# Signs of three pairs written as two halves side by side, and one pair's turns at slot 73

## The chip, the cores and the metric

One core of one Trainium2 chip. The metric is the device time of one execution in microseconds (us). Three runs of the kernel before took 329.01, 328.08 and 329.04 us, median 329.01. The engines are TensorE (PE, matrix products), VectorE (DVE), ScalarE (ACT), GpSimd (POOL) and SyncE (SP), which here only issues DMA transfers.

## What is computed

Attention under a hash mask, then a gated feed-forward layer on its result. In the reference, cut to what matters:

```python
q_bits = (einsum('bhsd,dk->bhsk', q, proj) > 0)      # 6 bits for each row; k_bits the same
mask = q_bucket[:, :, :, None] == k_bucket[:, :, None, :]
scores = where(mask, q @ k.T / sqrt(D), -1e9)
attn = softmax(scores) @ v                           # B=4, H=8, S=768, D=64
xn = rmsnorm(attn as rows of 512) * rms_g
out = (silu(xn @ w_gate) * (xn @ w_val)) @ w_out     # d_ff = 1536
```

The kernel writes the mask as arithmetic. Behind the 64 values of each k and q column of the tile QK stand 12 rows of bits, scaled so that one product over 76 rows gives the score of a pair of rows with equal buckets and a very negative number for all others.

## The kernel before

**Windows, pairs and slots.** The 3072 rows of the result are taken as eight windows w of 384 rows (batch b = w // 2). Heads go in pairs hp, so (b, hp) names the data of two heads. The work of attention is a list of 192 slots: one slot is one pair of score matmuls (`scores`, s_ps) and its exponentials on ACT (`probs`). Windows 0 to 3 take the pairs in the order of `TURNS`; the pairs of batch 1 come to their scores in the order (1,0), (1,1), (1,2), (1,3), six slots each, once for window 2 and once for window 3.

**The plan.** Everything else is entered by hand into a slot with `at(slot, function, ..., rank=...)`. The last loop walks through the slots, issues the scores of the next slot, and then the entries of this slot in the order of their rank (3 unless given). Each engine, and SP's queue of DMA issues, works through its own instructions in the order in which this loop issued them. An instruction that must wait holds up all that stand behind it on its engine.

**The feed-forward part of window w** begins at slot 24 w + 42: twelve gate steps (`gate`, g_ps, four matmuls and a tanh on ACT) and twelve value steps (`value`, v_ps, four matmuls and two DVE instructions t and ht) over 16 slots, then nine steps of the last product (`project`, y_ps). The tiles d_ps, g_ps, v_ps, m_ps, x_ps and y_ps go round three PSUM banks (pool `gps`): each allocation waits until the third one before it has been read.

**How q and k get to QK.** The first six pairs (`BY_PE`) are turned by PE. The others are loaded in blocks of 32 (`load_blocks`, four transfers for each of kL and qL, issued by SP) and turned by DVE in eight steps (`turn_dve`, L205: four of kT, then four of qT, one slot each, rank 5). `cast_pool` (L213) copies them to the rows 0 to 63 of QK on POOL.

**The hash.** `hash_bank` multiplies up to four 384-column blocks by the projection, each into its own strip of 32 partitions of one bank (d_ps, L221). `signs` (L228) turns a bank to bits on DVE, into a tile bits with three buffers. SP then sends rows of 12 partitions to the rows 64 to 75 of QK:

- `hash_heads` (slot 40 for pair (1,1)): strips are k and q of the first head, then of the second; `move` sends eight transfers (L279).
- `hash_lone` (slot 58 for (1,2), slot 65 for (1,3)): strips are k and q of the first half of the columns, then of the second; `send` issues four transfers for each head (L297), for (1,2) the second four at the end of slot 59.
- `hash_pairs` for two pairs of batch 2 or 3, two banks; pairs (2,0) and (2,1) at slot 82. It already writes the halves side by side and sends whole rows (L319).

**What else SP issues here:** the transposes of xn to xnT (`turn_x`, L458), the loads of q, k and v (L127, L117) and the stores of the result (L514).

**The table `work`** gives, for each pair turned by DVE, the slots of its loads of k, q and v, the first slot s of its eight turns, and the slot of its hash. The casts follow at s + 4 and s + 8, `v_prep` and `v_sum` at s + 9, and for (2,1) two slots later. Pair (2,1) has loads at 66, 67 and 68, turns from 74, hash at 82.

Of the kernel before, what the change touches and what calls it, by code (L numbers as in the profile page):

```python
# [9 lines left out]
FP16 = mybir.dt.float16  # L10
AF = mybir.ActivationFunctionType
ALU = mybir.AluOpType
# [4 lines left out]
S = 768  # L17
D = 64
# [3 lines left out]
HALF = 384  # L22
KROWS = D + 12
# [25 lines left out]
def kernel(  # L49
# [12 lines left out]
    nc = tc.nc  # L62
# [9 lines left out]
    spool = ctx.enter_context(tc.tile_pool(name="spool", bufs=2))  # L72
# [12 lines left out]
    thr = const.tile([128, 1], FP32, name="thr")  # L85
    scl = const.tile([128, 1], FP32, name="scl")
# [45 lines left out]
    T0, QK = {}, {}  # L132
# [16 lines left out]
    def t0(b, h, which):  # L149
        hp, hh = divmod(h, 2)  # L150
        return T0[b, hp, which][:, hh * HALF : (hh + 1) * HALF]
# [66 lines left out]
    def hash_bank(parts):  # L218
        ps = bank("d_ps", [128, HALF])
        for t, (w, src) in enumerate(parts):  # L220
            nc.tensor.matmul(  # L221
                ps[32 * t : 32 * t + 32, :], w, src,
                start=True, stop=True, tile_position=(0, 32 * t),
            )
        return ps

    def signs(bt, ps):
        nc.vector.tensor_scalar(  # L228
            out=bt, in0=ps, scalar1=thr, scalar2=scl, op0=ALU.is_gt, op1=ALU.mult
        )  # L230

    def bit_rows(b, h, t):
        return QK[b, h // 2][D:KROWS, h % 2, t * HALF : (t + 1) * HALF]

# [2 lines left out]
    def bits_tile(i):  # L237

        if i % 2 == 0:
            held.append(spool.tile([128, S], FP16, name="bits", bufs=3))  # L240
        return held[-1][:, (i % 2) * HALF : (i % 2 + 1) * HALF]

    def hash_head(h):


        kt, qt = t0(0, h, "k"), t0(0, h, "q")
        ps = hash_bank(
            [(pk[:, 0:32], kt), (pq[:, 0:32], qt), (pk[:, 12:44], kt), (pq[:, 12:44], qt)]
        )
        bt = bits_tile(h)  # L250
        signs(bt, ps)

        def move(movers, t0=0):
            for t, eng in enumerate(movers, t0):
                src = bt[32 * t : 32 * t + 12]
                if eng is nc.scalar:
                    nc.scalar.copy(bit_rows(0, h, t), src)
                elif eng is nc.sync:
                    eng.dma_start(out=bit_rows(0, h, t), in_=src)
                else:  # L260
                    eng.tensor_copy(bit_rows(0, h, t), src)

        return move

    def hash_heads(b, hp):

        ps = hash_bank(
            [(w[:, 0:32], t0(b, 2 * hp + hh, which))
             for hh in range(2) for w, which in ((pk, "k"), (pq, "q"))]
        )  # L270
        bt = bits_tile(0)
        signs(bt, ps)

        def move(eng, blocks):
            for hh, t in blocks:
                p0 = 64 * hh + 32 * (t % 2) + 12 * (t // 2)
                dst, src = bit_rows(b, 2 * hp + hh, t), bt[p0 : p0 + 12]
                if eng is nc.sync:
                    eng.dma_start(out=dst, in_=src)  # L279
                else:  # L280
                    eng.tensor_copy(dst, src)

        return move

    def hash_lone(b, hp):

        ps = hash_bank(
            [(w[:, 0:32], T0[b, hp, which][:, half * HALF : (half + 1) * HALF])
             for half in range(2) for w, which in ((pk, "k"), (pq, "q"))]
        )  # L290
        bt = bits_tile(0)
        signs(bt, ps)

        def send(hh):
            for half, j in ((0, 0), (0, 1), (1, 1), (1, 0)):
                p0, o = 64 * half + 32 * j + 12 * hh, (S, 0)[j] + half * HALF
                nc.sync.dma_start(  # L297
                    out=QK[b, hp][D:KROWS, hh, o : o + HALF], in_=bt[p0 : p0 + 12]
                )

        send(0)
        moves[b, hp] = send
# [324 lines left out]
    moves = {}  # L627
# [4 lines left out]

    def hash_pair(b, hp):
        moves[b, hp] = hash_heads(b, hp)
        odd = [(0, 2), (1, 2), (0, 3), (1, 3)]
        even = [(0, 0), (0, 1), (1, 0), (1, 1)]
        moves[b, hp](nc.sync, odd if b == 0 else even[:2] + odd[:1] + even[2:] + odd[1:])
# [17 lines left out]
    for hp, s, slots in ((2, 12, (13, 14, 15, 16)), (3, 17, (18, 19, 20, 21))):  # L655
        at(s, hash_pair, 0, hp)
        for i, s in enumerate(slots):
            at(s, lambda hp=hp, i=i: moves[0, hp](nc.vector, [divmod(i, 2)]), rank=5)
# [10 lines left out]
    for hp, loads, turns, sh, evens, sv in (  # L669
        (0, (9, 11, 13), (20, 21, 24, 27), 33, (41, 42), (27, 44)),  # L670
        (1, (13, 14, 36), (29, 31, 33, 35), 40, (45, 47), (49, 51)),
    ):
        for which, sl in zip("kqv", loads):
            at(sl, load_rows, nc.sync, 1, hp, which)
        for i, sl in enumerate(turns):
            at(sl, keep_pair, 1, hp, i)
            at(sl + 1, casts, 1, hp, i)
        at(sh, hash_pair, 1, hp)
        for hh, sl in enumerate(evens):
            at(sl, cast_half, 1, 2 * hp + hh, "q", 0)  # L680
        at(sv[0], v_prep, 1, hp)
        at(sv[1], v_sum, 1, hp)
# [3 lines left out]
    def in_row(loads, s, hash_slot=None):  # L686
        return loads, range(s, s + 8), (s + 4, s + 8, s + 9), hash_slot

    work = {
        (1, 2): in_row((31, 32, 45), 49, 58), (1, 3): in_row((41, 43, 50), 56, 65),  # L690
        (2, 0): in_row((53, 55, 60), 64), (2, 1): in_row((66, 67, 68), 74, 82),
        (2, 2): in_row((72, 75, 78), 82), (2, 3): in_row((79, 86, 87), 90, 99),
        (3, 0): in_row((88, 91, 98), 100), (3, 1): in_row((94, 97, 112), 110, 119),
        (3, 2): in_row((115, 118, 124), 126), (3, 3): in_row((122, 125, 137), 136, 145),
# [1 line left out]
    for (b, hp), (loads, turns, cast_slots, sh) in work.items():  # L696
        for which, s in zip("kqv", loads):
            at(s, load_rows if which == "v" else load_blocks, nc.sync, b, hp, which)
        for i, s in enumerate(turns):
            at(s, turn_dve, b, hp, "kq"[i // 4], i % 4, rank=5)  # L700
        for which, s in zip("kq", cast_slots):
            at(s, cast_pool, b, hp, which)
        if sh:
            later = {(1, 2): (59, 7), (2, 1): (86, 7)}.get((b, hp), (sh, 3))
            if b == 1:
                at(sh, hash_lone, b, hp)
            else:
                at(sh, hash_pairs, b, (hp - 1, hp))
            at(later[0], lambda b=b, hp=hp: moves[b, hp](1), rank=later[1])
        late = 2 if (b, hp) == (2, 1) else 0  # L710
        at(cast_slots[2] + late, v_prep, b, hp)
        at(cast_slots[2] + late, v_sum, b, hp)
        if b > 1 and hp % 2:
            at(48 * b + (17 if hp == 3 else -8), v_mean, b, hp - 1, 4)
# [27 lines left out]
    for w in range(8):  # L742
# [33 lines left out]
        for i in range(9 if w < 7 else 6):  # L776
            c, j = divmod(i, 3)
# [3 lines left out]
    for s in range(NS + 48):  # L781
# [3 lines left out]
        n = sum(r < 3 for r, _, _ in todo) if s < NS - 1 else 0  # L785
# [48 lines left out]
```

## Time and profile before

The profile is one execution taken by the hardware's profiler.

| | before |
|---|---|
| median of three runs | 329.01 us |
| the profiled execution | 328.34 us |
| its span in the trace | 326.6 us, 7743 instructions |
| PE busy | 98% of the span |
| DVE, ACT, POOL busy | 71%, 64%, 51% |
| granted clock of PE | 1.00 |
| chain that ended last | PE 92%, DVE 2%, ACT 2%, DMA 1% |

In a timeline a row is: start in us from the span's start, length in us, engine and line of the program, operation, the tile written <- the tiles read, shapes, and count; in brackets the idle time of the engine in front of it and what ended it. Rows with a count over 1 are merged, and neighbours on one engine can overlap a little. "SPq" is SP's queue of DMA issues: the length is that of the issue and not of the transfer. A row of the waits reads: engine, instruction <- what it waited for, then us in total, times, longest. A row of the windows has the stretch, its length, and for PE, weight loads, DVE, ACT and POOL the busy time with the number of instructions, then the granted clock, the share of the DMA engines and GB/s. A row for a tile has the line, engine, operation, count, and the shortest, median and longest duration in ns.

### The profile page before, as it was taken

The page shows a single profiled execution, that of the slowest core. Times are in us where ns is not written, and L with a number is a line of the kernel's source. Part 1 is how long each engine was busy: PE and PEld are TensorE (multiplying, and loading weights), DVE is VectorE, ACT ScalarE, POOL GpSimd, SP SyncE. Part 2 cuts the span into 40 slices and gives each one's busy share as a digit, 9 for nine tenths or more (in the row PEclk, how much of TensorE's full clock was granted, in tenths as well). Part 3 has the DMA queues.
Part 4 walks back from the last instruction along what each step waited for, and adds up shares of the span by engine and source line. Part 5 has one row for each costly group of instructions (what it writes and reads, how often), then busy time and mean ns, then how long its engine had stood idle before and what let it go on. Part 6 is the DMA issues. An engine that isn't in the chain of part 4 may idle for free.

```text
span 326.6 us, 7743 instructions
## 1 busy us (share of the span) xinstructions
PE 319.5 (98%) x2927; PEld 196.7 (60%) x2927; DVE 230.5 (71%) x514; ACT 208.2 (64%) x324; POOL 167.2 (51%) x238
## 2 busy tenths in 40 slices
PE   8999999999999999999999999999999999999995
PEld 7576766655566455656566656566566656655553
DVE  4798896789498885889387874968167734793860
ACT  3788986775576476657576766657677766423331
POOL 7887977279667686686934275733221320230000
PEclk9999999999999999999999999999999999999999
DMA  7998989985439935973460843002200021005002
GB/s 227 350 211 248 164 130 184 160 174 84 65 109 183 163 70 109 207 139 48 128 126 19 150 83 113 3 17 47 71 32 2 17 66 66 0 1 130 0 2 97
DMA packets 91269, 34.26 MB, mean 105 GB/s; under 512 B 76136, under 2 KB 88160, under 8 KB 91232
## 3 DMA queue, kind: packets, MB, share of 16 engines
q1 hardware_dynamic: 87152, 28.85, 38.7%
q0 software_dynamic: 3712, 4.72, 9.2%
q8 instruction: 23, 0.38, 0.5%
q10 hardware_dynamic: 368, 0.20, 0.2%
q14 instruction: 14, 0.11, 0.1%
HBM read 28.58 MB, written 6.29 MB: 107 GB/s over the span
## 4 chain that ended last, share of the span: by engine, by line
PE 92%; DVE 2%; ACT 2%; DMA 1%; issue 1%; POOL 0%; SPq 0%; DVEq 0%; ACTq 0%
PE v_ps L489 19%; PE y_ps L503 18%; PE s_ps L363 18%; PE g_ps L479 15%; PE o_ps L385 10%; PE d_ps L221 4%; PE s_ps L479 4%; PE t_ps L181 2%; ACT psb L373 1%; PE z_ps L356 1%; DMA QK<-bits 1%; DMA out_dram<-ysb 1%; DVE qT L205 1%; PE m_ps L344 1%; DVE t L490 0%
## 5 line engine op out<-in xcount | busy, mean ns | idle before, releaser
L373 ACT ACTIVATE psb<-s_ps 128x768 f16<-128x768 f32 x192 | 150.7, 809 | 30.5 <-PE s_ps L363 28.7
L363 PE MATMUL s_ps<-QK 128*128 128x384 f16 (+1 forms) x384 | 93.6, 326 | 1.1 <-ACT psb L373 0.3
L489 PE MATMUL v_ps<-xnT,wv 128*128 128x384 f16 x384 | 78.1, 326 | 0.0
L503 PE MATMUL y_ps<-wo,ht 128*128 128x512 f16 x276 | 68.9, 379 | 0.0
L490 DVE SCALAR_TENSOR_TENSOR t<-t,g_ps 128x384 f32<-128x384 f32 x78 | 42.9, 550 | 36.0 <-ACT t L481 35.8
L412 POOL TENSOR_TENSOR x<-otmp,rcp 128x384 f32<-128x384 f32 x30 | 25.7, 858 | 82.3 <-DVE rcp L405 82.1
L385 PEld LDWEIGHTS <-psb 128*128 128x128 f16 x1152 | 51.7, 98 | 22.0 <-issue 3.8
L481 ACT ACTIVATE t<-g_ps 128x384 f32<-128x384 f32 x78 | 38.3, 491 | 40.9 <-PE g_ps L479 37.3
L479 PE MATMUL g_ps<-xnT,wg 128*128 128x384 f16 x312 | 63.4, 326 | 0.0
L491 DVE SCALAR_TENSOR_TENSOR ht<-t,v_ps 128x384 f16<-128x384 f32 x96 | 53.2, 554 | 11.3 <-PE v_ps L489 1.2
L385 PE MATMUL o_ps<-vl,psb 128*128 128x65 f16 x1152 | 56.0, 193 | 0.0
L489 PEld LDWEIGHTS <-wv 128*128 128x128 f16 x384 | 36.5, 98 | 23.1 <-issue 0.3
L479 PEld LDWEIGHTS <-wg 128*128 128x128 f16 x384 | 36.1, 98 | 23.0
L503 PEld LDWEIGHTS <-ht 128*128 128x128 f16 x276 | 26.6, 98 | 27.6 <-issue 1.9
L363 PEld LDWEIGHTS <-QK 128*128 128x128 f16 (+1 forms) x384 | 31.1, 97 | 16.5 <-issue 3.1
L510 ACT COPY ysb<-y_ps 128x512 f32<-128x512 f32 x23 | 13.5, 586 | 22.3 <-PE y_ps L503 21.7
L400 DVE TENSOR_TENSOR otmp<-o_ps,cvb 128x390 f32<-128x390 f32 x32 | 17.8, 558 | 12.8 <-PE o_ps L385 12.8
L424 POOL TENSOR_TENSOR sq<-x 128x384 f32<-128x384 f32 x30 | 25.5, 848 | 2.4
L213 POOL CAST QK<-kT 64x768 f16<-64x768 f32 x20 | 17.0, 852 | 9.4 <-DVE kT L205 6.9
L213 POOL CAST QK<-qT 64x768 f16<-64x768 f32 x20 | 16.4, 820 | 9.8 <-DVE qT L205 9.0
L205 DVE STREAM_TRANSPOSE kT<-kL 128x192 f32<-128x192 f32 x40 | 19.5, 520 | 0.0
L205 DVE STREAM_TRANSPOSE qT<-qL 128x192 f32<-128x192 f32 x40 | 19.2, 520 | 0.0
(81 smaller groups left out, 296.4 us busy)
## 6 DMA issues: line engine op xcount, KB each, us to landing
vL<-in_v_dram SPq DMA_DIRECT2D x16, 384.0 KB
out_dram<-ysb SPq DMA_DIRECT2D x23, 256.0 KB
kL<-in_k_dram SPq DMA_DIRECT2D x40, 96.0 KB
qL<-in_q_dram SPq DMA_DIRECT2D x40, 96.0 KB
kL<-in_k_dram SPq DMA_DIRECT2D x5, 384.0 KB
qL<-in_q_dram SPq DMA_DIRECT2D x5, 384.0 KB
wg<-in_moe_w_gate_dram POOLq DMA_DIRECT2D x2, 768.0 KB, 8.5
wv<-in_moe_w_val_dram POOLq DMA_DIRECT2D x2, 768.0 KB, 9.0
```

Source lines behind the costliest of these rows:

```text
L205: nc.vector.transpose(dst.rearrange("p (c t r) -> p r c t", c=6, r=4)[:, r : r + 1], src.rearrange("p (r c) d -> p r c d", r=4)[:, r : r + 1],
L213: nc.gpsimd.tensor_copy(QK[b, hp][0:64, hh, o : o + S], T0[b, hp, which][64 * hh : 64 * hh + 64, :])
L363: nc.tensor.matmul(ps[:, j, 0:HALF], k_cols(w // 2, h, 2 * p + j), q_cols(w, h), start=True, stop=True,)
L373: nc.scalar.activation(psb[w, h][:, p], sps.pop(g)[:, :, 0:HALF], AF.Exp, scale=ESCALE,)
L385: nc.tensor.matmul(o[:, c, hh, 0:65], psb[w, h][:, jt // 2, jt % 2, 128 * c : 128 * c + 128], vls[b % 2][:, h, v_chunk(b, h, jt), 0:65], s ...
L412: eng.tensor_mul(xd.rearrange("p c (h d) -> p c h d", h=2), tmp[:, :, :, 0:64], r.to_broadcast([128, 3, 2, 64]),)
L479: nc.tensor.matmul(g, wg[:, kt, fs], xnT[w][:, kt], start=(kt == 0), stop=(kt == 3))
L481: nc.scalar.activation(t, g, AF.Tanh, scale=0.5)
L489: nc.tensor.matmul(vv, wv[:, kt, fs], xnT[w][:, kt], start=(kt == 0), stop=(kt == 3))
L490: nc.vector.scalar_tensor_tensor(out=t, in0=t, scalar=1.0, in1=g, op0=ALU.add, op1=ALU.mult)
L491: nc.vector.scalar_tensor_tensor(out=ht[w][:, ft], in0=t, scalar=0.5, in1=vv, op0=ALU.mult, op1=ALU.mult)
L503: nc.tensor.matmul(y, ht[w][:, ft, c * 128 : (c + 1) * 128], wo[:, ft, :], start=(ft == 0), stop=(ft == NF - 1),)
```

## The change

It does three things. A new function `signs_in_row` takes the place of `signs` for the pairs (1,1), (1,2) and (1,3): two DVE instructions of 64 partitions each, the second reading partitions 64 to 127 of the bank and writing partitions 0 to 63 of the bits tile, in the columns behind the first. The bits then lie side by side, so that these pairs are sent by four transfers and not by eight: for (1,1) each transfer has 12 partitions of both heads, for the other two 12 partitions of all 768 columns of one head. And the turns of pair (2,1) begin at slot 73, not 74, with its casts (77 and 81), `v_prep` and `v_sum` (84) one slot earlier too. `hash_pair` returns early for (1,1), since its transfers have been issued.

```diff
+    def signs_in_row(ps):
+
+        bt = spool.tile([128, S], FP16, name="bits", bufs=3)
+        for i in range(2):
+            p = slice(64 * i, 64 * i + 64)
+            nc.vector.tensor_scalar(
+                out=bt[0:64, i * HALF : (i + 1) * HALF], in0=ps[p], scalar1=thr[p],
+                scalar2=scl[p], op0=ALU.is_gt, op1=ALU.mult,
+            )
+        return bt
...
     def hash_heads(b, hp):
...
+        if (b, hp) == (1, 1):
+            bt = signs_in_row(ps).rearrange("p (h n) -> p h n", h=2)
+            for t in range(4):
+                p0 = 32 * (t % 2) + 12 * (t // 2)
+                nc.sync.dma_start(
+                    out=QK[b, hp][D:KROWS, :, t * HALF : (t + 1) * HALF], in_=bt[p0 : p0 + 12]
+                )
+            return None
         bt = bits_tile(0)
         signs(bt, ps)
...
     def hash_lone(b, hp):
...
-        bt = bits_tile(0)
-        signs(bt, ps)
+        bt = signs_in_row(ps)
 
         def send(hh):
-            for half, j in ((0, 0), (0, 1), (1, 1), (1, 0)):
-                p0, o = 64 * half + 32 * j + 12 * hh, (S, 0)[j] + half * HALF
-                nc.sync.dma_start(
-                    out=QK[b, hp][D:KROWS, hh, o : o + HALF], in_=bt[p0 : p0 + 12]
-                )
+            for j, o in enumerate((S, 0)):
+                p0 = 32 * j + 12 * hh
+                nc.sync.dma_start(out=QK[b, hp][D:KROWS, hh, o : o + S], in_=bt[p0 : p0 + 12])
...
     def hash_pair(b, hp):
         moves[b, hp] = hash_heads(b, hp)
+        if moves[b, hp] is None:
+            return
...
-        (2, 0): in_row((53, 55, 60), 64), (2, 1): in_row((66, 67, 68), 74, 82),
+        (2, 0): in_row((53, 55, 60), 64), (2, 1): in_row((66, 67, 68), 73, 82),
```

## The prediction

> **What bounds the kernel now.** I began with the page's busy times and the list of what TensorE (PE) waited for, then took ten-microsecond windows.
>
> ```profile
> PE 319.5 (98%) x2927; PEld 196.7 (60%) x2927; DVE 230.5 (71%) x514; ACT 208.2 (64%) x324; POOL 167.2 (51%) x238
> ```
>
> ```profile
> PE d_ps L221 <- DVE qT L205: 0.8, 1, 0.8
> ```
>
> ```profile
> 100.00:110.00 10.00, 10.00 (x95) 6.30 (x93) 9.32 (x23) 7.44 (x13) 6.64 (x8) 1.00 1.01 179
> 110.00:120.00 10.00, 9.24 (x83) 4.52 (x83) 8.03 (x15) 4.54 (x6) 7.59 (x10) 1.00 0.54 107
> ```
>
> PE is the bound, at a granted clock of 1.00, and the change takes no matmul from it. What can be gained is a wait of PE. Past slot 40, where the diff begins, the list has one of size: the hash matmuls (d_ps) waiting for a VectorE (DVE) transpose, in the stretch 110 to 120, behind ten microseconds in which DVE was 93% busy. That wait is the hash of pairs (2,0) and (2,1) in slot 82. Its timeline on PE:
>
> ```profile
> 109.98 0.51 PE L221 MATMUL d_ps<-kT,pk 128*32 128x384 f32 x1
> 109.98 0.51 PE L221 MATMUL d_ps<-qT,pq 128*32 128x384 f32 x1
> 109.99 0.82 PE L221 MATMUL d_ps<-kT,pk 128*32 128x384 f32 x2
> ...
> 111.58 0.51 PE L221 MATMUL d_ps<-qT,pq 128*32 128x384 f32 x1 [0.76 <-DVE qT L205]
> ...
> 112.25 0.81 PE L221 MATMUL d_ps<-qT,pq 128*32 128x384 f32 x2
> 112.99 1.04 PE L503 MATMUL y_ps<-wo,ht 128*128 128x512 f16 x4
> ```
>
> Three of the four column strips started at 109.98; the fourth, q of pair (2,1), started at 111.58. The idle time shown is 0.76 us, but more was lost: strips that start together run beside each other, and the late q strip of the first bank pushed the q strip of the second bank to the end, where it ran alone. What the same 16 records take without a wait stands at the next hash of two pairs:
>
> ```profile
> 139.76 0.51 PE L221 MATMUL d_ps<-kT,pk 128*32 128x384 f32 x1
> ...
> 141.19 0.50 PE L363 MATMUL s_ps<-QK 128*128 128x384 f16 x2
> ```
>
> From first hash matmul to the next work: 112.99 - 109.98 = 3.01 us with the wait, 141.19 - 139.76 = 1.43 us without. The wait costs 3.01 - 1.43 = **1.58 us**, twice its idle time.
>
> **Part one: the turns of pair (2,1) a slot earlier.** Eight transposes move from slots 74 to 81 to slots 73 to 80; each still stands last in its slot (rank 5), and so does its order against the others. DVE around them:
>
> ```profile
> 97.83 0.55 DVE L491 SCALAR_TENSOR_TENSOR ht<-t,v_ps 128x384 f16<-128x384 f32 x1
> 99.40 0.56 DVE L490 SCALAR_TENSOR_TENSOR t<-t,g_ps 128x384 f32<-128x384 f32 x1 [1.02 <-ACT t L481]
> ...
> 101.30 0.90 DVE L205 STREAM_TRANSPOSE kT<-kL 128x192 f32<-128x192 f32 x2
> ...
> 109.56 0.49 DVE L205 STREAM_TRANSPOSE qT<-qL 128x192 f32<-128x192 f32 x1
> 109.90 0.54 DVE L490 SCALAR_TENSOR_TENSOR t<-t,g_ps 128x384 f32<-128x384 f32 x1
> 110.54 0.56 DVE L491 SCALAR_TENSOR_TENSOR ht<-t,v_ps 128x384 f16<-128x384 f32 x1
> 111.01 0.51 DVE L205 STREAM_TRANSPOSE qT<-qL 128x192 f32<-128x192 f32 x1
> 112.45 1.32 DVE L228 TENSOR_SCALAR bits<-d_ps,thr,scl 128x384 f16<-128x384 f32 x2 [0.93 <-PE d_ps L221]
> ```
>
> The value steps of window 0 fall in slots 66 + (32 ft + 16) // 24, so the ht at 97.83 closes slot 73 and the t at 99.40 opens slot 74. Now the first transpose (0.51 us) comes between them, inside an idle time of 1.02 us that waits for ACT: it costs nothing there. From 99.40 on DVE has the same instructions in the same order, each transpose replaced by its successor, so all keep their times: the last q transpose takes the place of the one at 109.56 and ends at 110.05 in place of 111.52. PE followed the old one by 111.58 - 111.52 = 0.06 us, so the fourth strip could start at 110.11, where it is wanted at about 110.00: 0.11 us late. Gain: 1.58 - 0.11 = **1.47 us**.
>
> What is late next? The second bank and the first y_ps reuse banks that the t at 109.90 and the ht at 110.54 read last; they end at 110.44 and 111.10, and an undisturbed hash asks for them half-way and at its end, at 110.7 and 111.4 (109.98 + 1.43). Then comes window 2's gate, for which SP issues three transposes behind DVE's xn:
>
> ```profile
> 117.78 3.87 SPq L458 DMA_TRANSPOSE xnT<-xn  x3
> ```
>
> ```profile
> 125.15 0.81 PE L479 MATMUL g_ps<-xnT,wg 128*128 128x384 f16 x4
> ```
>
> ```profile
> 86.39 0.65 PE g_ps L479 x4
> ```
>
> Issue ends at 121.65. PE would come at 125.15 - 1.47 = 123.68. At window 1 the same issues ended at 84.32 (fence below) and the gate ran at 86.39, which leaves at most 2.1 us to land; even unmoved, xnT would be there at 123.7. It moves too, as the signs at 112.45 come earlier with the hash. So nothing takes back the gain here. The casts of the pair (slots 77 and 81) and its v_prep and v_sum (slot 84, one earlier too) stay in the same order among POOL's instructions, between the clears and the products of window 2, so POOL's order costs nothing.
>
> **Part two: the transfers.** The earlier first transpose wants kL of (2,1) at 98.4 and not at 101.30, so SP's queue matters.
>
> ```profile
> 53.88 6.09 SPq L279 DMA_DIRECT2D QK<-bits  x8
> ...
> 76.44 3.16 SPq L297 DMA_DIRECT2D QK<-bits  x4
> 79.71 4.61 SPq L458 DMA_TRANSPOSE xnT<-xn  x3
> 84.37 3.05 SPq L297 DMA_DIRECT2D QK<-bits  x4
> 87.53 0.46 SPq L117 DMA_DIRECT2D vL<-in_v_dram  x1
> 88.09 0.88 SPq L514 DMA_DIRECT2D out_dram<-ysb  x2
> 89.06 6.11 SPq L297 DMA_DIRECT2D QK<-bits  x8
> 95.21 3.36 SPq L127 DMA_DIRECT2D kL<-in_k_dram  x4
> ```
>
> SP issues without a pause from 53.88, 0.76 us for each bits transfer (6.09 / 8), and kL of (2,1), planned for slot 66 (that of the gate at 86.39), goes out at 95.21: ten microseconds late. A larger transfer costs no more to issue:
>
> ```profile
> L319 SPq DMA_DIRECT2D QK<-bits x32: 713/725/1077, 113.9 to 219.0; - x32
> L297 SPq DMA_DIRECT2D QK<-bits x16: 713/714/834, 76.4 to 94.5; - x16
> ```
>
> The rows of L319 carry twice the bytes. The two-head form of (1,1) has no row; between one issue (0.76) and two (1.52, nothing gained), I take one, as L319's doubled transfer does. Then everything behind these eight comes 4 x 0.76 = 3.0 us earlier, and SP reaches the bits of (1,2) at 73.4, where it must now wait for the signs (next part) until 75.4. Two sends to 77.0, three transposes to 81.6, two sends, a load and two stores to 84.7; wait for the signs of (1,3) to 85.4, four sends, and kL goes out at **88.5**, 6.7 us earlier. In the old run it was issued from 95.21 and read at 101.30 without a wait, so it lands within 6.1 us: by 94.6, well before 98.4. Queued behind the two waits are the transposes of window 1 (77.0, not 79.71) and these loads; all still start earlier than before. If the two-head form saves nothing, SP reaches the bits of (1,2) at 76.44, waits for no signs at all, and the same sum gives 88.8: the cover stays. Bits land sooner as well, but no score matmul waited for them, so that is worth nothing.
>
> **Part three: the signs in two halves.** Each of three pairs gets a second instruction, over 64 partitions and the same 384 elements.
>
> ```profile
> 48.41 0.67 DVE L228 TENSOR_SCALAR bits<-d_ps,thr,scl 128x384 f16<-128x384 f32 x1
> 50.05 0.56 DVE L490 SCALAR_TENSOR_TENSOR t<-t,g_ps 128x384 f32<-128x384 f32 x1 [0.98 <-ACT t L481]
> ...
> 74.17 0.59 DVE L228 TENSOR_SCALAR bits<-d_ps,thr,scl 128x384 f16<-128x384 f32 x1
> ...
> 77.24 1.11 DVE L447 SCALAR_TENSOR_TENSOR xn<-x,rstd,grow 128x512 f16<-128x512 f32 x1
> ...
> 84.03 0.68 DVE L228 TENSOR_SCALAR bits<-d_ps,thr,scl 128x384 f16<-128x384 f32 x1 [1.55 <-PE d_ps L221]
> ...
> 87.60 0.56 DVE L490 SCALAR_TENSOR_TENSOR t<-t,g_ps 128x384 f32<-128x384 f32 x1 [2.46 <-ACT t L481]
> ```
>
> No row has 64 partitions; bounds for one half are 0.34 us (half the work) and 1.36 us (twice, for reading one half of the partitions and writing the other), and I take 0.67, the row of the same free size. That is +0.67 us of DVE three times. At slot 40 the 0.98 us idle before 50.05 takes it; at slot 58 the idle time in front of the signs at 84.03 (1.55); at slot 65 that before 87.60 (2.46). Slot 58's has xn of window 1 behind it; the last of them ends at 78.35 + 0.67 = 79.0, and SP comes to its transpose only at 80.1 (the third of the three from 77.0), so it holds up nothing. The d_ps bank is held longer; the third allocation after it, where it comes round again, is the second g_ps of window 0, on PE at 50.31, and the bank is free at 48.41 + 1.34 = 49.75. Price: **0**. At the upper bound it would be 48.41 + 2.72 = 51.1, a wait of 0.8 us on PE.
>
> ```profile
> 50.31 0.81 PE L479 MATMUL g_ps<-xnT,wg 128*128 128x384 f16 x4
> ```
>
> [...]
>
> **The sum.** Turns -1.47, signs 0, transfers 0: the profiled execution took 328.34 us for a span of 326.6 and would take 326.87. The three runs have a median of 329.01, 0.67 above it; from that, 329.01 - 1.47 = **327.5 us**, 0.45% faster.
>
> **The rivals.** (a) *Only the idle time comes back.* If the lone last strip is no loss that order removes, the gain is 0.76 - 0.11 = 0.65 us: 328.4, inside 0.3%. The 1.43 against 3.01 us speaks against it. The same time comes if the signs meet their upper bound: 1.47 - 0.8 = 0.7. (b) *The turns come too early for their load (slower).* The first transpose stands in front of window 0's t at 99.40. If kL is not issued earlier and needs the whole 6.1 us, it runs at 101.30, t is pushed to 101.75 (half of the 0.90 for two) and DVE's full queue by 2.35 us; the last q transpose ends at 110.05 + 2.35 = 112.4, 0.9 us later than now, and PE with it: 329.9. It decides from a landing after 100.4, where 1.47 us of lateness has eaten the gain. SP's backlog speaks for it, the 6.7 us computed above against it. (c) *The stall returns elsewhere*, at the banks or window 2's gate, whose margins above are 0.3 us and about 0: the gain is halved, 328.3.
>
> **How the numbers follow.** A change under 0.3%, 1.0 us, can't be told from none here. Forecast 0.70; (a) 0.10 and (c) 0.08, both within; (b) 0.12. The likeliest one's own range is 326.5 (the lowest run less 1.58) to 327.9. To leave out no more than 2 in 10 the range goes up over (a) and (c), whose times stand up to the median: 326.4 to 329.2.
>
> **What would show it.** Right: no wait of PE for qT near 110; 16 hash matmuls of slot 82 within 1.6 us; first kT of (2,1) at 98.4 before the t at 99.4; kL issued at about 88.5; signs x21, 0.67 us each; 28 hash transfers to these three pairs and (1,0), (0,2), (0,3) where L279 and L297 now have 40. Wrong: a t that waits behind kT at 98 to 101, PE idle at 50 or at the gate of window 2, or a hash still near 3 us.

## The result

Six runs of the changed kernel took 325.70 to 326.51 us, median 325.87, beside six of the kernel before with a median of 328.99: a ratio of 0.9917, interval 0.9902 to 0.9931. The forecast was 327.5 us with a range from 326.4. The direction was right and the gain twice what was forecast. In a second set on another occasion the medians were 326.15 and 328.35 (ratio 0.9935, 0.9922 to 0.9949).

The page of the changed kernel, its engines and the chain that ended last:

```profile
span 324.0 us, 7728 instructions
...
PE 318.1 (98%) x2927; PEld 196.3 (61%) x2927; DVE 232.6 (72%) x517; ACT 208.2 (64%) x324; POOL 167.5 (52%) x238
...
PE 94%; DMA 2%; ACT 2%; DVE 0%; issue 0%; DVEq 0%; ACTq 0%
```

DVE has three instructions more and has left the chain (2% before). What PE waited for, the first four rows of the list:

```profile
PE z_ps L372 <- DVE pm L550: 1.0, 1, 1.0
PE s_ps L379 <- DMA QK<-bits: 0.4, 1, 0.4
PE s_ps L379 <- ACT psb L389: 0.3, 1, 0.3
PE s_ps L372 <- ACT psb L389: 0.2, 1, 0.2
```

The wait of d_ps for qT is gone. The wait for bits stands at 28 us, ahead of what the change touches, and PE has made it up by 32 us. The hash of slot 82 on PE's timeline:

```profile
109.70 0.51 PE L221 MATMUL d_ps<-kT,pk 128*32 128x384 f32 x1
109.71 0.51 PE L221 MATMUL d_ps<-qT,pq 128*32 128x384 f32 x1
109.72 0.51 PE L221 MATMUL d_ps<-kT,pk 128*32 128x384 f32 x1
109.81 0.51 PE L221 MATMUL d_ps<-qT,pq 128*32 128x384 f32 x1
...
111.22 1.04 PE L519 MATMUL y_ps<-wo,ht 128*128 128x512 f16 x4
```

All four strips start together, the last 0.10 us late, and the hash takes 111.22 - 109.70 = 1.52 us in place of 3.01. DVE and SP, in the stretches that the prediction worked on:

```profile
97.58 0.55 DVE L507 SCALAR_TENSOR_TENSOR ht<-t,v_ps 128x384 f16<-128x384 f32 x1
98.05 0.53 DVE L205 STREAM_TRANSPOSE kT<-kL 128x192 f32<-128x192 f32 x1
99.15 0.55 DVE L506 SCALAR_TENSOR_TENSOR t<-t,g_ps 128x384 f32<-128x384 f32 x1 [0.57 <-ACT t L497]
...
109.27 0.49 DVE L205 STREAM_TRANSPOSE qT<-qL 128x192 f32<-128x192 f32 x1
```

```profile
54.20 3.36 SPq L286 DMA_DIRECT2D QK<-bits  x4
...
74.87 1.67 SPq L315 DMA_DIRECT2D QK<-bits  x2
76.65 3.93 SPq L474 DMA_TRANSPOSE xnT<-xn  x3
...
85.17 3.08 SPq L315 DMA_DIRECT2D QK<-bits  x4
88.30 2.72 SPq L127 DMA_DIRECT2D kL<-in_k_dram  x4
```

The first transpose of (2,1) sits inside the idle time in front of t, the last one ends at 109.76, and kL is issued at 88.30 (88.5 was worked out). Up to here the trace is the one forecast. Where are the other microseconds? I laid PE's 2927 matmul records of the two executions side by side in their order and took the difference of the starts. That, and the stretch behind the last store, worked out from the records of the trace:

| stretch | before | after | difference |
|---|---|---|---|
| the first 6 us, up to the first hash matmul (start) | 5.91 | 5.65 | -0.26 |
| from there to slot 82 | | | -0.01 |
| hash of slot 82, to the last matmul (start) | 322.41 | 320.64 | -1.77 in all, -1.49 here |
| last matmul to the issue of the last store | 0.80 | 0.76 | -0.04 |
| issue of the last store to SP's last row (start) | 3.29 | 2.57 | -0.72 |

The first row comes from the granted clock and not from the change. The trace's records of it begin, at full clock, at 5.80 us before and at 4.66 after. The t_ps matmuls start every 0.21 us ahead of that mark and every 0.11 us behind it; before, and then after:

```profile
4.65 0.85 PE L181 MATMUL t_ps<-ident,qL 128*128 128x128 f32 x3
```

```profile
4.65 0.50 PE L181 MATMUL t_ps<-ident,qL 128*128 128x128 f32 x3
```

Over all twelve profiles the mark lies anywhere from 3.80 us (a kernel with the old signs) to 6.44 us (one with the new).

So 1.49 us came from the hash, and 0.72 us from a place that the prediction had not looked at: the end of the program, behind all work. SP's rows there, with their time since the issue of the last store (records of the trace):

```
before: issue 0 | waits 0.38 1.55 1.62 1.68 1.74 1.80 1.86 1.92 2.01 | drain 2.09 2.46 | 2.73 | 2.82 | 3.29
after:  issue 0 | waits 0.38 0.44 0.50 0.57 0.92 1.55 1.61 1.67 1.73 | drain 1.79 1.86 | 2.01 | 2.11 | 2.57
```

In both, the last store has landed at 1.55. Before, that is the second of nine waits, and seven rows of some 0.065 us stand behind it; after, it is the sixth, and three stand behind it. Between the two drains pass 0.37 us before and 0.07 us after. From the landing to the last row are 1.74 and 1.02 us.

### The profile page after: what moved, and what is told of

It is laid out like the page before. It is cut to its first block, busy times and chain, and to the rows that moved or that the text cites. A ratio compares the mean times of both kernels' runs of the same rounds, so it can differ in the third digit from the quotient of the medians.

```text
span 324.0 us, 7728 instructions
## 1 busy us (share of the span) xinstructions
PE 318.1 (98%) x2927; PEld 196.3 (61%) x2927; DVE 232.6 (72%) x517; ACT 208.2 (64%) x324; POOL 167.5 (52%) x238
## 4 chain that ended last, share of the span: by engine, by line
PE 94%; DMA 2%; ACT 2%; DVE 0%; issue 0%; DVEq 0%; ACTq 0%
PE v_ps L505 19%; PE s_ps L379 19%; PE y_ps L519 18%; PE g_ps L495 16%; PE o_ps L401 10%; PE d_ps L221 4%; PE s_ps L495 4%; PE t_ps L181 2%; DMA QK<-bits 2%; ACT psb L389 1%; PE z_ps L372 1%; DMA out_dram<-ysb 1%; PE m_ps L360 1%; PE x_ps L480 0%; DVE bits L228 0%
```

## The experiments

Theory: the turns give 1.5 us by ending the wait in slot 82, provided that SP's relief brings kL in time, and the number of transfers gives 0.7 us at the end. Rivals: SP's relief is the gain, or the end varies by itself.

**The turns back at slot 74, the rest of the change kept.**

```diff
-        (2, 0): in_row((53, 55, 60), 64), (2, 1): in_row((66, 67, 68), 73, 82),
+        (2, 0): in_row((53, 55, 60), 64), (2, 1): in_row((66, 67, 68), 74, 82),
```

> The changed kernel with the turns of (2,1) back at slot 74; signs in halves and fewer transfers stay. My theory: the wait of PE in slot 82 returns, some 0.7 us idle and a hash near 3.0 us, so the time is 1.5 us above the changed kernel, about 327.4, while the end of the program stays short (2.6 us from the issue of the last store to the end of the span). Rival: what gained was SP's queue and the earlier landing of bits, and the turns gained nothing: about 325.9.

Median 327.40 (11 runs; ratio to the kernel before 0.9962, 0.9940 to 0.9983). PE's timeline shows the old hash again:

```profile
109.98 0.51 PE L221 MATMUL d_ps<-kT,pk 128*32 128x384 f32 x1
...
111.55 0.51 PE L221 MATMUL d_ps<-qT,pq 128*32 128x384 f32 x1 [0.72 <-DVE qT L205]
...
112.96 1.04 PE L519 MATMUL y_ps<-wo,ht 128*128 128x512 f16 x4
```

112.96 - 109.98 = 2.98 us. Its matmuls keep the times of the kernel before to the end (last start 322.39 against 322.41), so the halved signs and the transfers are worth nothing to PE by themselves. Behind the last store it takes 2.56 us: the short end comes without the turns. The time is 1.25 us above the 326.15 of the changed kernel's second set, where 1.5 were expected; the last matmul stands 1.74 us later than the changed kernel's, 0.27 of it from the first microseconds.

**The turns alone, on the kernel before.**

```diff
-        (2, 0): in_row((53, 55, 60), 64), (2, 1): in_row((66, 67, 68), 74, 82),
+        (2, 0): in_row((53, 55, 60), 64), (2, 1): in_row((66, 67, 68), 73, 82),
```

> The kernel before with only the turns of (2,1) at slot 73; 128-partition signs and all transfers stay. kL of (2,1) is still issued from about 95.2 to 98.6, and its first reader comes at 98.4. If the transfers are needed as cover, the first transpose waits for the load to about 100.4 or later, DVE is late by 1 to 2 us up to the hash, and the time is 328.5 to 329.5, nothing gained or worse. Rival: the load lands within 1 us of its last issue and the turns alone bring the whole 1.5 us: about 327.4, with the end of the program as long as before (3.3 us).

Median 328.42 over twelve runs from 327.07 to 329.40: no gain (0.9992, 0.9968 to 1.0016), and a spread of 2.3 us. The profiled one was the fastest. Its DVE:

```profile
99.48 0.53 DVE L205 STREAM_TRANSPOSE kT<-kL 128x192 f32<-128x192 f32 x1 [1.09 <-DMA kL<-in_k_dram]
99.85 0.54 DVE L490 SCALAR_TENSOR_TENSOR t<-t,g_ps 128x384 f32<-128x384 f32 x1
```

Here SP happened to issue kL at 93.79; the transpose waited until 99.48, t was late by 0.45 us, and the hash still had its four strips together. By the last matmul it was 1.26 us ahead of the kernel before. Two more profiles of the same kernel were to show one of the longer times.

> The kernel before with only the turns at slot 73, a second profile, since its twelve times lay between 327.1 and 329.4 us. The first profile, a fast one, had kL issued from 93.8, landed at 99.5, and DVE idle for 1.1 us in front of the first transpose. My theory: the slow ones have kL landing after 100.4 and a hash that waits for qT as in the kernel before. If this is a slow one (328.5 or more), DVE waits for kL for 2 us or more; if a fast one (327.5 or less), 1.2 us or less. Rival: the times differ for something outside 95 to 112 us.

> The same kernel, a third profile, with the same expectation: the later kL lands, the longer DVE waits and the longer the time.

They took 330.17 and 328.95 us. In the first of them kL was issued at 95.13, as in the kernel before, DVE waited 3.0 us, and PE, behind it, for t:

```profile
101.04 0.52 DVE L205 STREAM_TRANSPOSE kT<-kL 128x192 f32<-128x192 f32 x1 [3.02 <-DMA kL<-in_k_dram]
```

```profile
102.00 0.81 PE L489 MATMUL v_ps<-xnT,wv 128*128 128x384 f16 x4 [1.29 <-DVE t L490]
103.23 0.55 PE L385 MATMUL o_ps<-vl,psb 128*128 128x65 f16 x9 [0.42 <-DVE otmp L400]
103.59 1.47 PE L479 MATMUL g_ps<-xnT,wg 128*128 128x384 f16 x4
```

In the other, issue was at 95.72, the transpose at 101.36 and PE's waits 1.10 and 0.42 us. DVE's waits, 3.0 us in both, were as expected, and the expected hash that waits for qT did not come. DVE had caught up by then, and in the first of the two the hash ran like this:

```profile
113.29 0.51 PE L221 MATMUL d_ps<-kT,pk 128*32 128x384 f32 x1
...
113.41 0.51 PE L221 MATMUL d_ps<-qT,pq 128*32 128x384 f32 x1
...
114.81 1.04 PE L503 MATMUL y_ps<-wo,ht 128*128 128x512 f16 x4
```

That is 1.52 us again. Against the kernel before, PE's matmuls in both fall behind by 2.0 us at the waits near 102 and gain 1.5 and 1.6 us back in the hash; in the first, 1.6 us more are lost while the granted clock is down (last section). At the last matmul the two are 1.83 and 0.61 us late. In the three profiles the load took 5.6 to 5.9 us from its first issue to the transpose that waited for it. The turns at 73 without SP's relief gain when kL happens to go out early and lose when it does not, as rival (b) had it, but the loss falls on v_ps behind t, and not on the hash.

**Four transfers more, on the kernel before.**

```diff
-                nc.sync.dma_start(out=rows[:, out_chunk(w, c), :], in_=ysb)
+                cuts = (0, 256, DMODEL) if (w, c) in ((4, 0), (4, 1), (4, 2), (5, 0)) else (0, DMODEL)
+                for lo, hi in zip(cuts, cuts[1:]):
+                    nc.sync.dma_start(out=rows[:, out_chunk(w, c), lo:hi], in_=ysb[:, lo:hi])
```

> The kernel before with four stores of windows 4 and 5 each sent as two halves: four more transfers, all other work as before. My theory of the part not foreseen (0.7 us behind the last store): SP waits at the end for eight transfer semaphores in a fixed order, and transfers take the eight in turn, so the number of transfers decides how many waits stand behind that of the last store. Four more move it from the first to the fifth place, as in the changed kernel: the stretch from the issue of the last store to the end of the span falls from 3.3 to 2.6 us and the time by 0.3 to 0.7 us, although work was added. Rival: the stretch varies from run to run and has nothing to do with the count: 3.3 us again, or a value that does not follow the place.

Behind the last store it took 2.92 us: neither 2.6 nor 3.3. Three waits stood behind the landing, as worked out, but with a pause among them:

```
e5: issue 0 | waits 0.38 0.44 0.50 0.57 0.87 1.55 1.94 2.02 2.08 | drain 2.15 2.22 | 2.37 | 2.46 | 2.92
```

From 1.55 to 1.94 are 0.39 us and not 0.065. The pause that lay between the drains before (0.37) lies four rows nearer to the last store here, where four transfers were added: in both it stands in front of the 336th row of SP's queue. The changed kernel has 327 rows in that queue and never gets there. The time was 328.36 (0.9992, 0.9973 to 1.0012); 0.37 us are too few to be told in it.

**Three transfers more, on the changed kernel** (the same edit for the three stores of window 4).

> The changed kernel with three stores of window 4 each sent as two halves. My theory: the last store's semaphore moves to the last place, no wait stands behind it, and the stretch from its issue to the end of the span is 0.2 us shorter than the 2.6 of the changed kernel, 2.4. Rival: 2.6, or above for the added transfers.

2.39 us behind the last store: the wait for it is the last of the nine, and the next row is the drain. With 330 rows no pause. Time 326.22 (11 runs), not to be told from the 326.15 of the changed kernel's second set.

**Twelve transfers more, on the changed kernel,** so that SP has as many as before (the same edit for all stores of windows 2 to 5).

> The changed kernel with the twelve stores of windows 2 to 5 sent as halves, so that SP issues as many transfers as before. My theory: the last store's semaphore is first in the list again (7 waits of 0.065 us behind it, 0.3 us more than with 3), and SP's queue is long enough again to meet the pause of 0.3 us that stands at its 336th row in each of the three kernels that are so long. So the stretch behind the last store is 3.3 us and the time 0.7 us above the changed kernel, while PE's last matmul keeps its time. Rival: the stretch is short because of what the change does to the bits, and stays at 2.6.

3.28 us behind the last store, with the rows of the kernel before to within 0.02 us, the pause between the drains included. The last matmul started at 320.92, 0.27 us after the changed kernel's, a shift that stands from the first microseconds on. Median 326.74 against 326.15 of the changed kernel in the same set: +0.59 us. The end goes with the number of SP's transfers: of the change, nothing else was taken back here.

**The signs twice.**

```diff
-        for i in range(2):
+        for i in (0, 1, 0, 1):
```

> The changed kernel with each of the two sign instructions issued twice, writing the same values: +1.36 us of DVE in slots 40, 58 and 65. If the idle time named in the prediction hides the halves but no more, the bank at slot 40 comes free at about 50.9 and not 49.5, PE's second g_ps of window 0 waits some 0.8 us for it, and slots 58 and 65 stay free of charge: 0.8 us above the changed kernel. If DVE's backlog at slot 58 reaches the transposes of window 1, more: 1.5 to 2.5 us. If nothing shows, the halves had a wider cover than I gave them.

Median 327.00, 0.85 us above the changed kernel. DVE and PE at slot 40:

```profile
48.59 2.80 DVE L237 TENSOR_SCALAR bits<-d_ps,thr,scl 64x384 f16<-64x384 f32 x4
```

```profile
51.44 0.81 PE L495 MATMUL g_ps<-xnT,wg 128*128 128x384 f16 x4 [0.74 <-DVE bits L237]
```

The bank comes free at 51.39 and PE waits 0.74 us for it; at slots 58 and 65 nothing. The cover at slot 40 is that bank: the halves fit in front of its next use (free at 49.52, used at 50.06), the doubled ones overrun it.

**The changed kernel and the kernel before once more.**

> The changed kernel once more, beside the ones below. The end of its matmuls should stand 1.5 us ahead of the kernel before, give or take the 0.3 us by which the first microseconds differ from run to run, and the stretch behind the last store should be 2.6 us again. If the 3.1 us between the medians were the change's own, this set shows it again; if part of it was the scatter of the six runs before, it comes out at 2.2 to 2.6.

> The kernel before once more, for a second profile. If its scatter (327.8 to 331.8 us) comes from loads and bits that land late behind SP's backlog, a slow one shows a wait for a transfer on DVE, POOL or PE between 60 and 115 us; if from the first microseconds, the matmuls up to 10 us stand shifted by up to 0.9 us and keep that shift.

Five of six runs of the changed kernel lay between 325.76 and 326.49, and the difference of the medians was 2.20 us, the lower end of what was expected. The sixth took 328.61, and that one was profiled: at 28 us PE waited 1.5 us for bits of batch 0, ahead of anything that the change touches.

```profile
29.59 0.65 PE L379 MATMUL s_ps<-QK 76*128 76x384 f16 x3 [1.51 <-DMA QK<-bits]
```

The kernel before took 328.21 in the median of eight; in the profiled execution its matmuls are up to 0.3 us ahead of its first profile in the first 6 us, and 0.17 us of that stays to the last one. None of its longer executions (up to 331.8 us) was caught in a profile, so the cause of its scatter stays open.

## Why the prediction was right and where it was wrong

**The wait in slot 82** was right in kind and size. It was read as 1.58 us, twice its idle time, with 0.11 us to be left; 3.01 - 1.52 = 1.49 us came back and the last strip was 0.10 us late. Rival (a), that only the idle time of 0.76 us returns, is out: the two half-empty passes of the strips were a cost of the wait.

**The room for the first transpose** was right: the idle time of 1.02 us shrank to 0.57, and DVE's order behind it kept its times (109.27 against 109.56, all but 0.02 us of it the shift that PE has from the first microseconds).

**SP's relief as cover** was right, and needed. 6.7 us of lead were worked out and 6.9 were seen (95.21 to 88.30), 0.27 of them the same shift. Without it the time went as rival (b) said, and not the way it said. The break-even, put at a landing after 100.4, fits: landings at 101.0 and 101.4 lost and one at 99.5 gained. But (b) had DVE late to the end of its queue and the hash 0.9 us late by it. In the two profiles PE itself waited for t and fell 2.0 us behind, DVE was back in time for the hash, and 0.6 us were lost at the end where the clock stayed up. Two readings on the way were off: kL went out 8.8 us behind its slot before (95.21 against 86.39) and not ten, and the relief at (1,1) was 2.7 us (6.09 to 3.36) and not 3.0. The two-head form of (1,1) takes one issue of 0.78 us, not two. The signs, for the next paragraph, and these transfers:

```profile
L237 DVE TENSOR_SCALAR bits<-d_ps,thr,scl x6: 585/677/685, 48.2 to 84.5; 64x384 f16<-64x384 f32 x6
L286 SPq DMA_DIRECT2D QK<-bits x4: 779/788/870, 54.2 to 56.8; - x4
```

**The signs at nothing** was right: 0.677 us for a half, near the 0.67 taken between 0.34 and 1.36, and hidden in all three places. The row of a transpose before, and three rows after:

```profile
84.62 0.52 DVE L205 STREAM_TRANSPOSE kT<-kL 128x192 f32<-128x192 f32 x1
```

```profile
83.77 1.37 DVE L237 TENSOR_SCALAR bits<-d_ps,thr,scl 64x384 f16<-64x384 f32 x2 [1.52 <-PE d_ps L221]
85.18 0.53 DVE L205 STREAM_TRANSPOSE kT<-kL 128x192 f32<-128x192 f32 x1
87.35 0.55 DVE L506 SCALAR_TENSOR_TENSOR t<-t,g_ps 128x384 f32<-128x384 f32 x1 [1.64 <-ACT t L497]
```

At slot 65 the idle time fell from 2.46 to 1.64 us, by 0.82 and not by 0.67, and the transpose starts only after the signs have ended (83.77 + 1.37 = 85.14); before, it started 0.09 us ahead of their end (84.03 + 0.68 = 84.71). The 0.15 us between 0.82 and 0.67 are mostly this: 0.09 us ahead of the end then and 0.04 behind it now. The same idle time hid them. Why the transpose waits for the end of the halves, the trace does not show.

**The transfers at nothing** is the step that failed. "Turns -1.47, signs 0, transfers 0" priced twelve transfers fewer by what waits for them in the middle of the program, and never looked at the end of the span, where SP's nine waits hold the eight transfer semaphores in one order in both traces: 100, 102, then 104 to 109. The last store has 100 before (the second wait) and 106 after (the sixth). The term is -0.72 us: 0.29 from four waits fewer behind the landing, 0.31 from the pause that the shorter queue does not reach, and 0.12 in the step behind the drains, where the drain behind the pause takes 0.12 us and not 0.01. The range repeats the step: its lower end, 326.4, is the lowest run less the whole wait (326.5) and next to nothing for a gain elsewhere, and every rival was slower than the forecast.

**The base** was a choice that cost nearly as much again. From the profiled execution, 328.34 - 1.47 - 0.72 = 326.15, the median of the second set; less the 0.26 us of the first microseconds, 325.89, where the profiled execution of the changed kernel took 325.82. I took the median of three runs, 329.01, as the base, 0.67 higher. With the missing term it gives 329.01 - 1.47 - 0.72 = 326.82, still 0.95 above the measured 325.87. The other two sets of the kernel before, 35 and 15 runs, have 328.33 and 328.35. The gain that all parts explain is 2.2 us. The first set's 3.1 holds 0.9 us that did not return in the second: there the kernel before was 0.64 us faster and the changed one 0.28 us slower. What that was, no profile shows.

## What to carry to other kernels

A wait inside a group of matmuls that run beside each other can cost more than its idle time, here 1.49 us for 0.76: compare the group with an undisturbed one. A step may be moved ahead only as far as its load allows (with kL landing at 101.0 and 101.4 us the same turns lost, at 99.5 they gained), so the queue that issues the load belongs to the same change, and the two have to be tried apart to see it. A count of transfers can be worth something at the end of the program, here 0.72 us: read the rows behind the last store before a price of zero is given.

## What the runs showed of the hardware

The pause of 0.3 us in SP's queue stood in front of its 336th row in the two profiles of the kernel before, in the three with the turns alone, in the one with four and in the one with twelve transfers more; the cause isn't seen in the trace.

In two executions a wait of PE of over a microsecond cost about its length again. After the 1.29 us (and 0.42) of the turns alone, and after the 1.51 us of the disturbed run of the changed kernel, the trace's records show a granted clock of 0.50 for 3.41 us. The windows ahead of the fall and in it, for the two:

```profile
99.98:103.39 3.41, 1.70 (x15) 0.78 (x14) 2.21 (x6) 1.90 (x3) 0.03 (x2) 1.00 0.98 130
103.39:106.80 3.41, 3.41 (x20) 1.68 (x17) 2.61 (x6) 1.30 (x2) 3.21 (x4) 0.50 1.02 261
```

```profile
27.80:31.21 3.41, 1.60 (x20) 0.99 (x17) 2.08 (x4) 1.46 (x3) 2.76 (x4) 1.00 0.95 311
31.21:34.62 3.41, 3.41 (x25) 2.69 (x24) 2.38 (x6) 2.08 (x4) 1.14 (x2) 0.50 1.03 172
```

In the first, four g_ps matmuls took 1.47 us and not 0.81, and in both PE fell behind by some 1.6 us more. The waits of 0.76 us in slot 82 and 0.74 us with the signs doubled left the clock at 1.00, and so did the 1.10 and 0.42 us of the third profile of the turns alone, where PE was busy for 1.89 of 3.41 us:

```profile
100.86:104.27 3.41, 1.89 (x19) 0.98 (x17) 2.77 (x8) 1.90 (x3) 0.56 (x1) 1.00 0.94 126
```

Ahead of both falls PE was busy for about half of the 3.41 us, for 1.70 and 1.60. Whether a limit of that busy time lies between 1.70 and 1.89 us, or something else decides, no run here shows.
